# Recurrent attention and a sine feed-forward on one core: turns of three tiles moved next to other small matrix work, fewer output products ahead of phase 1, another order of loads

## The chip, the cores and the metric

One core of a Trainium2 chip runs the kernel. The metric is device time in microseconds (us), the median of several executions; lower is better. Engines are named as in the profile: PE is TensorE (matrix products; PEld its weight loads), DVE is VectorE, ACT is ScalarE, POOL is GpSimd, SP is SyncE, which issues transfers only. GpSimd issues most of the loads as well. PSUM is the memory into which TensorE writes, and a tile there must be emptied before its buffer is used again.

## The reference

```python
gamma = 1.0 - 2.0 ** (-5.0 - np.arange(H))            # B, H, S, D = 4, 8, 768, 64
for t in range(S):
    state = gamma * state + k[:, :, t] (x) v[:, :, t]   # outer product, 64 x 64 per head
    y[:, :, t] = D ** -0.5 * q[:, :, t] @ state
x = y.transpose(0, 2, 1, 3).reshape(3072, 512)
h = x @ w_in                                           # 512 -> 2048
g = h + sin(alpha * h) ** 2 / (alpha + 1e-9)
out = g @ w_out                                        # 2048 -> 512
```

All inputs are float32; the kernel converts them to bfloat16 while they are loaded.

## The kernel before, in words

**Tiles.** The recurrence is computed in chunks of 128 tokens, six for each of the four batch rows, 24 tiles in all. `order` (also `P`) lists them: first the four first chunks (`e0` to `e3`, which need no earlier state), then chunks 1 to 5 of batch row 0 (`P[4]` to `P[8]`), of row 1 (`P[9]` to `P[13]`), and so on. Tiles form ten groups of 4, 2, ..., 2, 4, and the feed-forward takes one group at a time (`sizes`, line 50).

**A tile's attention.** Its q and k are *turned* (transposed) first: by TensorE in `stage_T` (line 259), with one copy out of PSUM by the engine given, or from `P[8]` on by a transfer on SP's queue (`turn`, line 272). Its v is multiplied by decays in place (`scale_v`, line 154). Then comes its *stretch* on TensorE, `burst(old, new)` (line 413): `inter` (q of the old tile times the state in `s_q`), a first round of products over the old tile's own scores and values, the `scores` of the new tile, and a second round, which a `nop` holds back until the first is written (`behind`). Tiles from the middle of row 1 on (`wide`) have another layout: their state products are in `sums` and their own products in `mix`. The stretch leaves closures that other engines run later: `exit` (DVE multiplies the result into `xT`), `keep` (DVE adds to the state `s_f`), `hand` (ACT or POOL copies `s_f` into `s_q` for the next stretch) and `mask` (DVE masks the scores of the new tile into `aT`). `first_state` (line 291) builds the state of batch row 0 behind its first chunk.

**The feed-forward.** `Slot` (line 484) computes some columns of h for a group (16 matmuls of 128 x 128 weights, four for each 128 columns of `d_ff`), ACT takes the sine, `sq` squares it on ACT or DVE, `add` (DVE) writes `gT`. `ff_out` (line 520) accumulates one of 16 products (`po`) of `g @ w_out` for one tile; `take` copies a finished output and SP stores it. `F` calls it for the tiles 0 to 2 of the first group, `fill(n)` takes the next n from a list of 26 products of the tiles 2 and 3 of that group, `outs`; what is left of the list goes into phase 1, spread over its slots.

**Order.** Nothing is scheduled for the author: each engine executes its instructions in the order of the text, and each waits by semaphores for its data. The text runs: loads on POOL's queue (lines 160 to 174 and 615 to 626), the first chunks' attention, phase 0 (lines 675 to 711: slots of the first group, with `F` behind them), a bridge (lines 712 to 762: the attention of `P[4]` and `P[5]`, the turns of `P[4]` to `P[6]`, the rest of `F`, fills, and in the middle POOL's list of later loads and scales), and then `phase(g, ...)` for the groups 1 to 9, in which the stretches and turns are hung at places `(group, slot)`. In phase 1 the turn of `P[7]` hangs at slot 0, the stretches of `P[6]` and `P[7]` at the slots 2 and 5 of eight.

PSUM is shared by tags: `mm` (four buffers: slots, turns, outputs), `pa` (scores) and `two` (one double bank: stretches and, early on, two outputs).

Of the kernel before, what the change touches and what calls it, by code (L numbers as in the profile page):

```python
# [16 lines left out]
def kernel(  # L17
# [15 lines left out]
    nc = tc.nc  # L33
    B, H, S, D = q.shape
    C = 128
    NCH = S // C
# [33 lines left out]
    def half(x):  # L70
        return slice(64 * x, 64 * x + 64)
# [94 lines left out]
    for b in range(2):  # L166
        nc.gpsimd.iota(tok[64 * b:64 * b + 64], pattern=[[C, NCH], [64, 2]], channel_multiplier=1, base=0,
                       allow_small_or_imprecise_dtypes=True)
    load_chunk(order[3], "qk")
    for h in range(2):  # L170
        load_w_out(0, h)
    load_chunk(order[3], "v")
    load_w_in(1)
    load_w_out(1)

# [115 lines left out]
    def first_state(j):  # L291

        ps = psum.tile([128, NP, D], F32, name="ps", tag="mm", bufs=4)
        for b, m, e in heads:
            h = head(b, m, e)
            nc.tensor.matmul(ps[half(e), 2 * b + m, :], raw["k", j][:, h, :], raw["v", j][:, h, :],
                             start=(b == 0 and m == 0), stop=True, skip_group_check=True)
        nc.scalar.copy(s_q[1], ps)
        nc.vector.tensor_copy(s_f, ps)

# [64 lines left out]

    def sums(now, to, lo):

        ks, vs = raw["k", now], raw["v", now]
        for r in range(2):
            for b, m, e in heads:  # L370
                if wide(now):
                    bank, at, kh, vh = b, lo, ks[half(b), r, 2 * m + e, :], vs[half(b), r, 2 * m + e, :]
                else:
                    h, f = head(b, m, e), b ^ r
                    bank, at, vh = f, lo + 128 * r, vs[half(f), h, :]
                    kh = ks[half(f), h, :]
                last = nc.tensor.matmul(to[bank][half(e), at + 64 * m:at + 64 * m + 64], kh, vh,
                                        start=False, stop=True, skip_group_check=True)
        return last
# [33 lines left out]
    def burst(old, new, first=None, apart=False):  # L413
# [4 lines left out]
        if not wide(old):  # L418
            last = round_of(old, now, 0)
        elif now is not None and now is not old:  # L420
            last = sums(now, st["py", old], 256)
        more = scores(new) if new is not None else {}
        py = st["py", old]
        at = [t[:, 256:384] for t in py]
        if wide(old) and now is old:
            pa = st["pa", new]
            at = [pa[:, b, 384:512] for b in range(2)]
            sums(now, [pa[:, b] for b in range(2)], 384)
        rest = tiles4
        if new is None:  # L430
# [17 lines left out]
        def keep():  # L448
            if wide(old) and now is not old:
                nc.vector.tensor_copy(s_f.rearrange("p (b m) d -> p b m d", b=2),  # L450
                                      st["pyw", old][:, :, 256:384].rearrange("p b (m d) -> p b m d", m=2))
                for b in range(2):
                    o = s_f[:, 2 * b:2 * b + 2]
                    nc.vector.tensor_add(o, o, py[1 - b][:, 384:512].rearrange("p (m d) -> p m d", m=2))  # L454
                return
# [157 lines left out]
    for j in (e0, e1):  # L613
        scale_v(j, nc.vector)
    for h in range(2):
        load_w_in(2, h)
    for c in range(1, NCH - 1):
        decay_table(c)
    load_w_out(2)
    for h in range(2):  # L620
        load_w_in(3, h)
    load_chunk(order[4], "qk")
    load_w_out(3)
    load_chunk(order[4], "v")
    for j in order[5:7]:
        load_chunk(j)

# [43 lines left out]
    def fill(n):  # L671
        for _ in range(n):
            outs.pop(0)()
# [14 lines left out]
    c.add()  # L688
    stage_M(e3, psum.tile([128, 2, 512], F32, name="pye", tag="pa")[:, 0])
    d.add()  # L690
    for j in (e2, e3):
        scale_v(j, nc.vector)
    F((0, 1, 2), (2,))
# [4 lines left out]
    for f in range(5, FF):  # L698
# [9 lines left out]
        if f == 9:  # L708
            first_state(e0)
        if f == 13:  # L710
            stage_T(P[4], nc.vector, "pa")
    scale_v(P[4], nc.gpsimd)
    m4 = scores(P[4])["mask"]
    F((0, 1), (13,))
    fill(5)
    stage_T(P[5], nc.scalar, "mm")
    a.add()
    m4()
    fill(3)
    scale_v(P[5], nc.vector)  # L720
    fresh = burst(P[4], P[5], apart=True)
    run(fresh, "keep", "hand", "mask")
    fill(2)
    F((0, 1), (14,))
    F((0, 1), (15,))
    run(fresh, "exit")


    load_chunk(P[7])
    load_chunk(P[8], "qk")  # L730
    scale_v(P[6], nc.gpsimd)
# [3 lines left out]
    load_chunk(P[10], "qk")  # L735
    decay_table(NCH - 1)
    load_chunk(P[9], "v")
    scale_v(P[8], nc.gpsimd)
    load_chunk(P[10], "v")
    load_seq(1, "q")  # L740
    load_seq(1, "k")
    load_seq(1, "v")
    scale_v(P[10], nc.gpsimd)
    load_seq(2, "q")
# [11 lines left out]
    load_seq(3, "v")  # L756

    fill(1)
    stage_T(P[6], nc.scalar, "mm")
    fill(3)  # L760
    run(burst(P[5], P[6]), "exit", "keep", "hand", "mask")
    fill(4)
    where = {7: (1, 2), 8: (1, 5)}
# [12 lines left out]

    at((1, 0), lambda: stage_T(P[7]))
    for n in (8, 9):
        at((1, n - 7), X(P[n]))
    for n in range(7, NJ + 1):  # L780
# [5 lines left out]
        if n >= 19 and n < NJ:  # L786
            at(where[n], lambda j=new: scale_v(j, nc.gpsimd))
    at((2, 3), lambda: scale_v(P[9], nc.vector))
    phase(1, outs, atts[1], 2)
    for g in range(2, NG):  # L790
# [32 lines left out]
```

## Time and profile before

| | us |
|---|---|
| median of three runs | 210.12 (209.93 to 210.23) |
| the profiled execution | 209.51 |
| its span in the profile | 207.7 |
| TensorE busy | 198.0 (95%) |
| VectorE, ScalarE, GpSimd busy | 152.8, 151.5, 116.3 |
| software queue of transfers (GpSimd's) | 92.1% of 16 engines' span |

The page of the profile has the busy times, the span in 40 slices of 5.2 us (a digit is a busy share in tenths), and groups of instructions. A row of a timeline has the start in us, the us that a merged run of like instructions covers, engine, line, operation, output and inputs, shapes and count, and in brackets the idle time before it with what ended it. Matrix products are pipelined, so the next row begins before the covered time of a row is over: the distance of two starts is the cost. The trace lacks a few records of `po` directly behind stretches; an idle time of 0.16 us with "issue" that is printed there is such a missing product.

### The profile page before, as it was taken

The page shows a single profiled execution, that of the slowest core. Times are in us where ns is not written, and L with a number is a line of the kernel's source. Part 1 is how long each engine was busy: PE and PEld are TensorE (multiplying, and loading weights), DVE is VectorE, ACT ScalarE, POOL GpSimd, SP SyncE. Part 2 cuts the span into 40 slices and gives each one's busy share as a digit, 9 for nine tenths or more (in the row PEclk, how much of TensorE's full clock was granted, in tenths as well). Part 3 has the DMA queues.
Part 4 walks back from the last instruction along what each step waited for, and adds up shares of the span by engine and source line. Part 5 has one row for each costly group of instructions (what it writes and reads, how often), then busy time and mean ns, then how long its engine had stood idle before and what let it go on. Part 6 is the DMA issues. An engine that isn't in the chain of part 4 may idle for free.

```text
span 207.7 us, 5741 instructions
## 1 busy us (share of the span) xinstructions
PE 198.0 (95%) x2342; PEld 123.4 (59%) x2370; DVE 152.8 (74%) x314; ACT 151.5 (73%) x309; POOL 116.3 (56%) x157
## 2 busy tenths in 40 slices
PE   7799999999999999999999999999999999999994
PEld 2445544457766666666666666666666654444453
DVE  5789788867989967868878868868888965656220
ACT  7778776657998787687687687686685779999001
POOL 8999956699999999898499932002022300000000
PEclk9999999999999999999999999999999999999999
DMA  8999999999999999999999996421422101010212
GB/s 134 152 181 197 202 200 183 154 168 198 156 161 113 110 189 155 171 103 161 114 141 197 159 172 71 104 70 35 106 63 41 54 2 52 0 50 3 101 50 101
DMA packets 102074, 24.79 MB, mean 119 GB/s; under 512 B 93040, under 2 KB 99104, under 8 KB 102048
## 3 DMA queue, kind: packets, MB, share of 16 engines
q0 software_dynamic: 79248, 13.38, 92.1%
q1 hardware_dynamic: 22656, 10.99, 26.0%
q8 instruction: 18, 0.29, 0.6%
q14 instruction: 8, 0.07, 0.1%
q10 hardware_dynamic: 144, 0.07, 0.1%
HBM read 27.30 MB, written 6.29 MB: 162 GB/s over the span
## 4 chain that ended last, share of the span: by engine, by line
PE 85%; ACT 5%; DVE 3%; DMA 2%; issue 2%; POOL 2%; POOLq 0%; ACTq 0%
PE po L523 37%; PE ph L498 37%; DMA qkr<-in_q_dram 2%; PE py L338 2%; ACT s L501 2%; ACT s L506 2%; PE poh L548 2%; PE py L392 1%; DVE gT L513 1%; DVE aT L288 1%; PE pt L266 1%; POOL vr L100 1%; POOL qkr L100 1%; PE pa L348 1%; PE pa L355 1%
## 5 line engine op out<-in xcount | busy, mean ns | idle before, releaser
L513 DVE SCALAR_TENSOR_TENSOR gT<-s,rec_alpha,ph 128x256 bf16<-128x256 f32 (+3 forms) x164 | 79.9, 523 | 30.9 <-ACT s L506 30.4
L498 PE MATMUL ph<-xT,w_in 128*128 128x256 bf16 (+3 forms) x652 | 98.3, 290 | 0.5 <-issue 0.3
L501 ACT ACTIVATE s<-ph,alpha_sb 128x256 f32<-128x256 f32 (+3 forms) x164 | 76.0, 506 | 29.9 <-PE ph L498 29.9
L523 PE MATMUL po<-w_out,gT 128*128 128x512 bf16 x345 | 90.5, 379 | 3.1 <-issue 2.7
L498 PEld LDWEIGHTS <-w_in 128*128 128x128 bf16 x656 | 63.3, 98 | 33.1 <-issue 1.0
L506 ACT ACTIVATE s<-s 128x512 f32<-128x512 f32 (+1 forms) x91 | 56.9, 625 | 2.9
L523 PEld LDWEIGHTS <-gT 128*128 128x128 bf16 x368 | 34.0, 98 | 30.3 <-DVE gT L513 0.2
L535 DVE COPY o_sb<-po 128x512 f32<-128x512 f32 x20 | 13.8, 690 | 10.3 <-PE po L523 9.8
L469 POOL CAST s_q<-s_f 128x256 bf16<-128x256 f32 x5 | 2.0, 396 | 34.2 <-DVE s_f L454 17.8
L120 POOL DMA_DIRECT2D qk_seq<-in_q_dram x24 | 17.0, 808 | 3.5 <-DMA v_seq<-in_v_dram 3.4
L120 POOL DMA_DIRECT2D qk_seq<-in_k_dram x24 | 17.1, 779 | 1.1 <-DMA qk_seq<-in_q_dram 0.7
L120 POOL DMA_DIRECT2D v_seq<-in_v_dram x24 | 16.9, 802 | 0.0
L158 POOL TENSOR_TENSOR v_seq<-v_seq,kgq 128x512 bf16<-128x512 bf16 x13 | 13.7, 1075 | 3.8 <-DMA v_seq<-in_v_dram 3.8
L443 DVE TENSOR_TENSOR xT<-py,qg 128x512 bf16<-128x512 f32 x19 | 13.0, 684 | 0.6 <-PE py L408 0.6
L363 DVE TENSOR_TENSOR aTw<-pa,maskq 128x768 bf16<-128x768 f32 x13 | 12.4, 952 | 0.0
L100 POOL DMA_DIRECT2D vr<-in_v_dram x11 | 10.2, 929 | 0.9 <-DMA w_in<-in_moe_w_in_dram 0.5
L552 ACT COPY o_sb<-poh 128x256 f32<-128x256 f32 (+1 forms) x2 | 0.6, 319 | 11.7 <-PE poh L548 11.2
L568 PE MATMUL spare<-warm 128*128 128x512 bf16 x24 | 7.7, 450 | 1.2 <-DVE warm L178 1.2
L351 DVE TENSOR_TENSOR aT<-pa,mask 128x1024 bf16<-128x1024 f32 x7 | 8.5, 1219 | 0.0
L469 ACT CAST s_q<-s_f 128x256 bf16<-128x256 f32 x14 | 5.5, 391 | 3.3 <-DVE s_f L463 3.0
L158 POOL TENSOR_TENSOR vr<-vr,kg 128x512 bf16<-128x512 bf16 x5 | 5.6, 1126 | 2.9 <-DMA vr<-in_v_dram 2.8
L100 POOL DMA_DIRECT2D qkr<-in_k_dram x7 | 6.3, 898 | 1.7 <-DMA w_out<-in_moe_w_out_dram 1.7
(101 smaller groups left out, 162.1 us busy)
## 6 DMA issues: line engine op xcount, KB each, us to landing
out_dram<-o_sb SPq DMA_DIRECT2D x23, 256.0 KB, 3.7
w_in<-in_moe_w_in_dram POOLq DMA_DIRECT2D x6, 256.0 KB, 9.9
w_out<-in_moe_w_out_dram POOLq DMA_DIRECT2D x3, 512.0 KB, 10.5
vr<-in_v_dram POOLq DMA_DIRECT2D x11, 128.0 KB, 5.4
qk_seq<-in_q_dram POOLq DMA_DIRECT2D x16, 80.0 KB, 7.8
qk_seq<-in_k_dram POOLq DMA_DIRECT2D x16, 80.0 KB, 5.6
v_seq<-in_v_dram POOLq DMA_DIRECT2D x16, 80.0 KB, 5.1
qkr<-in_q_dram POOLq DMA_DIRECT2D x7, 128.0 KB, 5.3
```

Source lines behind the costliest of these rows:

```text
L100: nc.gpsimd.dma_start(out=t, in_=chunk_of(src, j))
L120: nc.gpsimd.dma_start(out=o, in_=src[bt, head(b, m, e), cs[0] * C:, :].rearrange("(f i) d -> i f d", i=64))
L158: eng.tensor_mul(t, t, by[:, j % NCH, :, None].to_broadcast([128, H, D]))
L351: return {"mask": lambda: nc.vector.tensor_mul(aT.rearrange("p e n t -> p (e n) t"), pa.rearrange("p e (n t) -> p (e n) t", n=NP), mask_bc)}
L363: return {"mask": lambda: nc.vector.tensor_mul(aT, pa[:, :, 0:384].rearrange("p e (m t) -> p e m t", m=2), maskq[:, None, None, :].to_broa ...
L443: nc.vector.tensor_mul(o, st["pyw", old][:, :, 0:256].rearrange("p b (m t) -> p b m t", m=2), by)
L498: nc.tensor.matmul(self.ph[:, m, :], w_in[:, i, f * 128:(f + 1) * 128], xT[g][:, i, self.lo:self.hi], start=(m == 0 and i == 0), stop=(i = ...
L501: nc.scalar.activation(out=self.s[:, m, :], in_=self.ph[:, m, :], func=ACTF.Sin, scale=alpha_sb[:, f:f + 1])
L506: nc.scalar.activation(out=self.s, in_=self.s, func=ACTF.Square)
L513: nc.vector.scalar_tensor_tensor(gT[self.g][:, f, self.lo:self.hi], self.s[:, m, :], rec_alpha[:, f:f + 1], self.ph[:, m, :], op0=ALU.mult ...
L523: nc.tensor.matmul(po[g, ts], gT[g][:, f, ts * C:(ts + 1) * C], w_out[:, f, :], start=(f == 0), stop=(f == FF - 1))
L535: nc.vector.tensor_copy(o_sb, po[g, ts])
```

## The change

- **Loads.** `w_out`'s first half, then the v of `e3`, then the other half; the second quarters of both weights and the third of `w_in` in halves, in turn. The fifth decay table is built with the other four. The last quarter of `w_out` goes ahead of `P[4]`; the q and k of `P[5]` and `P[6]` go ahead of their v. The q and k of `P[7]` and `P[8]` are issued ahead of the scale of `P[5]`, the v of `P[7]` behind it.
- **First state.** Its eight products stand behind `stage_M(e3)`, its two copies behind `d.add()`; `scale_v(e3)` takes the old place at slot 9.
- **Turns.** `P[4]`'s goes from slot 13 to the end of phase 0; `P[5]`'s stands directly behind `P[4]`'s scores, `P[6]`'s and `P[7]`'s directly behind the stretches of `P[4]` and `P[5]`, all three copied by ACT.
- **Fills.** 11 of the 26 products are taken ahead of phase 1 instead of 18.
- **Scales.** `P[5]`'s goes from DVE to POOL, `P[10]`'s from POOL to DVE (phase 3, slot 0).
- **Rounds.** Where a `wide` stretch crosses into the next batch row, half of the first-state products go behind the scores, into the scores' PSUM tile.

```diff
@@ -167,11 +167,14 @@
         nc.gpsimd.iota(tok[64 * b:64 * b + 64], pattern=[[C, NCH], [64, 2]], channel_multiplier=1, base=0,
                        allow_small_or_imprecise_dtypes=True)
     load_chunk(order[3], "qk")
+    load_w_out(0, 0)
+    load_chunk(order[3], "v")
+    load_w_out(0, 1)
     for h in range(2):
-        load_w_out(0, h)
-    load_chunk(order[3], "v")
-    load_w_in(1)
-    load_w_out(1)
+        load_w_in(1, h)
+    for h in range(2):
+        load_w_out(1, h)
+        load_w_in(2, h)
     warm = consts.tile([128, 512], BF16, name="warm")
@@ -289,14 +292,16 @@
-        nc.scalar.copy(s_q[1], ps)
-        nc.vector.tensor_copy(s_f, ps)
+        def copies():
+            nc.scalar.copy(s_q[1], ps)
+            nc.vector.tensor_copy(s_f, ps)
+        return copies
@@ -363,16 +368,16 @@
-    def sums(now, to, lo):
+    def sums(now, to, lo, rs=(0, 1)):
...
-        for r in range(2):
+        for r in rs:
...
-                    bank, at, vh = f, lo + 128 * r, vs[half(f), h, :]
+                    bank, at, vh = f, lo, vs[half(f), h, :]
@@ -418,7 +423,7 @@
-            last = sums(now, st["py", old], 256)
+            last = sums(now, st["py", old], 256, (0,))
@@ -426,6 +431,8 @@
+        elif wide(old) and now is not None:
+            sums(now, [st["pa", new][:, b] for b in range(2)], 384, (1,))
@@ -451,7 +458,7 @@
-                    nc.vector.tensor_add(o, o, py[1 - b][:, 384:512].rearrange("p (m d) -> p m d", m=2))
+                    nc.vector.tensor_add(o, o, st["pa", new][:, 1 - b, 384:512].rearrange("p (m d) -> p m d", m=2))
@@ -612,18 +619,17 @@
     later_mask()
     for j in (e0, e1):
         scale_v(j, nc.vector)
-    for h in range(2):
-        load_w_in(2, h)
-    for c in range(1, NCH - 1):
+    for c in range(1, NCH):
         decay_table(c)
     load_w_out(2)
     for h in range(2):
         load_w_in(3, h)
-    load_chunk(order[4], "qk")
     load_w_out(3)
-    load_chunk(order[4], "v")
+    load_chunk(order[4])
     for j in order[5:7]:
-        load_chunk(j)
+        load_chunk(j, "qk")
+    for j in order[5:7]:
+        load_chunk(j, "v")
     rest = [{}]
@@ -687,9 +693,10 @@
     F((0, 1, 2), (0, 1))
     c.add()
     stage_M(e3, psum.tile([128, 2, 512], F32, name="pye", tag="pa")[:, 0])
+    copies = first_state(e0)
     d.add()
-    for j in (e2, e3):
-        scale_v(j, nc.vector)
+    copies()
+    scale_v(e2, nc.vector)
     F((0, 1, 2), (2,))
     a = Slot(0, 0, (n3, n4), 4, "pa")
     F((0, 1, 2), (3,))
@@ -706,41 +713,38 @@
         if f > 6:
             F((0, 1, 2) if f < 9 else (0, 1), (f - 3,))
         if f == 9:
-            first_state(e0)
-        if f == 13:
-            stage_T(P[4], nc.vector, "pa")
+            scale_v(e3, nc.vector)
     scale_v(P[4], nc.gpsimd)
+    load_chunk(P[7], "qk")
+    load_chunk(P[8], "qk")
+    stage_T(P[4], nc.vector, "pa")
+    F((0, 1), (13,))
+    fill(4)
+    a.add()
     m4 = scores(P[4])["mask"]
-    F((0, 1), (13,))
-    fill(5)
     stage_T(P[5], nc.scalar, "mm")
-    a.add()
     m4()
-    fill(3)
-    scale_v(P[5], nc.vector)
-    fresh = burst(P[4], P[5], apart=True)
-    run(fresh, "keep", "hand", "mask")
-    fill(2)
     F((0, 1), (14,))
     F((0, 1), (15,))
-    run(fresh, "exit")
-    load_chunk(P[7])
-    load_chunk(P[8], "qk")
+    fill(1)
+    scale_v(P[5], nc.gpsimd)
+    fresh = burst(P[4], P[5], apart=True)
+    stage_T(P[6], nc.scalar, "mm")
+    run(fresh, "keep", "hand", "mask", "exit")
+    load_chunk(P[7], "v")
     scale_v(P[6], nc.gpsimd)
     load_chunk(P[9], "qk")
     load_chunk(P[8], "v")
     scale_v(P[7], nc.gpsimd)
     load_chunk(P[10], "qk")
-    decay_table(NCH - 1)
     load_chunk(P[9], "v")
     scale_v(P[8], nc.gpsimd)
-    load_chunk(P[10], "v")
     load_seq(1, "q")
     load_seq(1, "k")
+    load_chunk(P[10], "v")
     load_seq(1, "v")
-    scale_v(P[10], nc.gpsimd)
     load_seq(2, "q")
     scale_v(P[11], nc.gpsimd)
     load_seq(2, "k")
@@ -755,11 +759,11 @@
         scale_v(j, nc.gpsimd)
     load_seq(3, "v")
+    fill(5)
+    fresh = burst(P[5], P[6])
+    stage_T(P[7], nc.scalar, "mm")
+    run(fresh, "exit", "keep", "hand", "mask")
     fill(1)
-    stage_T(P[6], nc.scalar, "mm")
-    fill(3)
-    run(burst(P[5], P[6]), "exit", "keep", "hand", "mask")
-    fill(4)
     where = {7: (1, 2), 8: (1, 5)}
     for g in range(2, NG - 1):
         first = P.index(groups[g + 1][0])
@@ -774,7 +778,6 @@
-    at((1, 0), lambda: stage_T(P[7]))
@@ -786,6 +789,7 @@
+    at((3, 0), lambda: scale_v(P[10], nc.vector))
```

## The prediction

> **What bounds the kernel now.** I read the page first, then TensorE's own waits, then the chain of waits for the price of one matrix instruction, then the timelines of TensorE and GpSimd from 14 to 61 us, where every edit but one falls.
>
> ```profile
> span 207.7 us, 5741 instructions
> ...
> PE 198.0 (95%) x2342; PEld 123.4 (59%) x2370; DVE 152.8 (74%) x314; ACT 151.5 (73%) x309; POOL 116.3 (56%) x157
> ...
> DMA  8999999999999999999999996421422101010212
> ```
>
> TensorE is busy for 198.0 of 207.7 us, so a gain must take away matrix work or one of its few gaps. The DMA row says something else about the first quarter: from the second slice on, the transfer engines are full for over 100 us. A load there lands when the bytes ahead of it have gone through, whatever the time of its issue.
>
> ```profile
> 5.06 4.85 DMA qkr<-in_q_dram
> ...
> 19.51 0.53 DVE gT L513
> ...
> 71.38 0.87 PE ph L498 x8
> ...
> 190.47 9.28 PE po L523 x43
> ```
>
> From the chain: a 256-column `ph` costs 0.87/8 = 0.109 us, a `po` 9.28/43 = 0.216 us. A pair of rows that lies further apart than these prices hides a wait even where no idle time is printed. That is how the next rows are read.
>
> **The change, part by part.** The profiled execution took 209.51 us (span 207.7, 1.8 around it); the median shown is 210.12, 0.6 above. I sum against 209.51 and add the 0.6 at the end.
>
> *First state beside stage_M.*
>
> ```profile
> 19.59 0.41 PE L314 MATMUL pye<-aT,vr 128*64 128x128 bf16 x8
> 20.09 0.82 PE L523 MATMUL po<-w_out,gT 128*128 128x512 bf16 x3
> ...
> 29.32 0.32 PE L296 MATMUL ps<-vr,kb 128*64 128x64 bf16 x8
> 29.57 1.04 PE L498 MATMUL ph<-xT,w_in 128*128 128x512 bf16 x4
> ```
>
> The `po` at 20.09 waited for VectorE's add, 19.51 + 0.53 = 20.04. The eight `ps` matmuls take 29.57 - 29.32 = 0.25 us, and 0.09 to enter (below). Behind `stage_M`, in the same 128*64 shape, they fill that wait, which costs nothing; if the wait were gone they would cost 0.25 there. The gain is 0.34 at 29 us (bounds 0.09 and 0.34). ScalarE's and VectorE's two copies move with them into a stretch where VectorE also loses one `scale_v`.
>
> *Turns next to scores and stretches.*
>
> ```profile
> 40.08 0.64 PE L266 MATMUL pt<-ident,qkr 128*64 128x128 bf16 x16
> ...
> 45.42 0.28 PE L401 MATMUL py<-aT,vr 64*64 64x128 bf16 x8
> 45.48 0.28 PE L408 MATMUL py<-vr,qkr 64*64 64x64 bf16 x8
> 45.70 0.42 PE L348 MATMUL pa<-qkT 64*64 64x128 bf16 x16
> ...
> 47.17 1.03 PE L498 MATMUL ph<-xT,w_in 128*128 128x256 bf16 x8
> 48.13 0.64 PE L266 MATMUL pt<-ident,qkr 128*64 128x128 bf16 x16
> 48.70 0.39 PE L523 MATMUL po<-w_out,gT 128*128 128x512 bf16 x1
> ```
>
> Eight `ph` from 47.17 end at 48.04, the turn starts at 48.13: 0.09 to enter. The turn then holds TensorE 0.57, so a turn on its own costs 0.66. Merged, it drops the entry and the exit of one of the two (taken as long as an entry, for want of a row), 0.18 for each of three; no row shows 64*64 followed by 128*64, so the saving lies between 0 and 0.18. The Trainium skill ("TensorEngine Tiling (Array Packing)", Key Properties) says that changing the tiling mode drains TensorE, so a turn behind a stretch would still pay one drain, and three merges would give about 0.27 instead of 0.54 us.
>
> In that second stretch eight L401 matmuls took 0.06, the eight L408 behind them 0.22: the scores of P[6] (45.70) had to wait for ScalarE's copy of its turn, which was only just out (44.64 + 1.01 = 45.65):
>
> ```profile
> 42.98 0.40 ACT L469 CAST s_q<-s_f 128x256 bf16<-128x256 f32 x1 [1.20 <-DVE s_f L463]
> ...
> 44.64 1.01 ACT L268 COPY qkT<-pt 128x1024 bf16<-128x1024 bf16 x1 [0.20 <-PE pt L266]
> ```
>
> That is a hidden wait of about 0.12, and it goes, as the turn moves ahead.
>
> *What is late next.* These savings count only if TensorE need not wait for loads and scaled values.
>
> ```profile
> 16.77 4.03 POOL L231 TENSOR_TENSOR qg<-qg,step 128x512 f32<-128x512 f32 x4
> 20.75 0.82 POOL L135 DMA_DIRECT2D w_out<-in_moe_w_out_dram  x1
> ...
> 27.50 0.87 POOL L100 DMA_DIRECT2D qkr<-in_q_dram  x1 [0.43 <-DMA w_in<-in_moe_w_in_dram]
> 30.05 0.87 POOL L100 DMA_DIRECT2D qkr<-in_k_dram  x1 [1.67 <-DMA w_out<-in_moe_w_out_dram]
> ...
> 38.23 1.04 POOL L158 TENSOR_TENSOR vr<-vr,kg 128x512 bf16<-128x512 bf16 x1 [2.85 <-DMA vr<-in_v_dram]
> ...
> 41.01 0.90 POOL L100 DMA_DIRECT2D vr<-in_v_dram  x1
> 41.88 1.53 POOL L98 DMA_DIRECT2D qkr<-in_q_dram  x2
> 43.35 1.54 POOL L98 DMA_DIRECT2D qkr<-in_k_dram  x2
> 44.84 1.12 POOL L158 TENSOR_TENSOR vr<-vr,kg 128x512 bf16<-128x512 bf16 x1
> ```
>
> ```profile
> qkr<-in_k_dram POOLq DMA_DIRECT2D x1, 128.0 KB, 10.0
> ```
>
> The k of P[5] (issued at 30.05) lands 10.0 us later, at 40.05; its turn ran at 40.08. In the changed order exactly the same loads precede it (all weights, P[4], its own q), so with full transfer engines it lands at 40.05 again. TensorE would come to that turn at 40.08 - 0.34 (first state) - 0.22 (one `po` fewer ahead) - about 0.1 (scores joined) = 39.4 and wait 0.6 us. The first gains are lost there.
>
> The second gate is GpSimd. The v of P[4] lands at 38.23, again behind the same loads. Then GpSimd scales it, issues q and k of P[7] and the four pieces of P[8], and only then scales P[5], which VectorE did before. Before, the v of P[7] stood between (41.88 - 41.01 = 0.87) and the scale behind the four pieces began at 44.84: now it begins at 43.97 and ends at 45.09 (bounds 45.0 and 45.3 by other durations of this operation, 1.04 and 1.31). The second stretch's round over P[5]'s values can start at 45.15; in the run before it started at 45.42. What is queued behind it on TensorE is the whole rest, since it executes in order. TensorE would be there at about 44.5: the T[5] turn at 40.08 holds it 0.57, five `po` 1.08, the stretch about 0.9 (below: 1.75 less four `po` and the wait, and 0.14 ahead of its round), the turn 0.57, five `po` 1.08, entries 0.2. ScalarE gives nearly the same limit: P[6]'s turn is copied (1.01) ahead of the state's hand-over (0.40), from about 43.3 to 44.7.
>
> From that round to the first slot of phase 1 it was 47.17 - 45.42 = 1.75 us, of it 0.12 the wait for the copy; the rest hangs on VectorE's exit and stays. So phase 1 begins at 45.15 + 1.63 = 46.78, 0.39 sooner.
>
> *What phase 1 then carries.* Fifteen `po` instead of eight: + 7 x 0.216 = 1.51. Its turn at slot 0 is gone: -0.66. Its gaps:
>
> ```profile
> 57.60 2.14 PE L498 MATMUL ph<-xT,w_in 128*128 128x256 bf16 x16
> 59.63 1.02 PE L523 MATMUL po<-w_out,gT 128*128 128x512 bf16 x4
> 60.62 1.03 PE L498 MATMUL ph<-xT,w_in 128*128 128x256 bf16 x8
> ```
>
> Sixteen `ph` should take 1.74 and took 2.03; four `po` 0.86 and took 0.99. These 0.42 us are ScalarE's pace at the end of phase 1; with 1.5 us more of `po` between the slots and sines that start 0.4 sooner they go: -0.42 (bounds 0 and 0.42).
>
> *First-state rounds apart*, in the two stretches that cross into a new batch row.
>
> ```profile
> 101.23 0.20 PE L359 MATMUL pa<-qkT 64*64 64x64 bf16 x4
> 101.45 0.37 PE L392 MATMUL py<-aTw,v_seq 64*64 64x128 bf16 x16
> ```
>
> The mix begins 0.22 after the last scores have begun, although four such matmuls take 0.03: it waits until the sums are written. With half of the sums (eight of 16, 0.06) behind the scores, that half covers part of the wait: -0.06 each, -0.12 for both (bounds 0 and -0.4).
>
> *Moved at no cost:* `scale_v(e3)` to the tenth slot of phase 0 (VectorE idles there), P[10]'s scale from GpSimd to VectorE one slot before its stretch, the v of P[7] and P[10] later on GpSimd's queue by 4 and 1 us, still several us ahead of their rounds. If one of these covers failed, it would cost the 0.7 us of one scale.
>
> *The sum:* -0.39 + 1.51 - 0.66 - 0.42 - 0.12 = -0.08 us, so 209.4 for the profiled execution and **210.0** as a median.
>
> **The rivals.** *A, the forecast: the gates hold.* Its own range: the landing of P[4]'s v moves everything one to one; I allow half a transfer of 128 KB (0.87 by the spacing 41.88 - 41.01) to either side, 0.45, and the bounds above: 209.5 to 210.7.
>
> *B, the gates lie earlier and the covers do their work.* Then TensorE's own sum decides: -0.34 (first state), -0.12 (the wait for the copy), -0.54 (three merges), -0.42, -0.12 = -1.54, that is 208.6. It needs P[5]'s k 0.65 us sooner, and its scaled v well over 1 us sooner. For it: loads that are cut finer and reordered could run better than in the profile, and the turn at 40.08 shows that P[5] was already at the limit, so each tenth sooner counts in full. Against it: the full DMA row. Half of it, 209.3, is as likely as all.
>
> *C, slower: the transfer queue runs dry behind the decay tables.* Weights in halves mean two more issues (0.75 each) ahead of the tables, and the tables are five instead of four (1.0 each): the next weight is issued at 20.75 + 2.5 = 23.3. What is queued by then lasts until the second half of `w_in`'s third quarter has landed, about 27.3 (the issue at 27.50 had waited for it), so 4.0 us. A load with some others ahead took 4.85 from issue to landing at the start of the run. If a new issue needs more than 4.0 us, the rest leaves a hole, up to 0.85 us, which shifts P[4]'s v, P[5]'s k and so everything behind: 210.9. It decides from a hole of 0.5 on. Against it: before, an equal pause in issues left no dip in the DMA row. The Trainium skill ("DMA: Bandwidth & Descriptors", Anatomy of one DMA) gives about 2.0 us of fixed time for such a load, by which the queue would not run dry and C would be out.
>
> **How the numbers follow.** A 0.42, B 0.32, C 0.26. What a measurement here can tell is about 0.2%, 0.42 us. A is faster by more in some 0.08, slower in 0.03, the same in the rest: faster 0.40, same 0.31, slower 0.29. The range leaves out the far end of B and what lies above C's price: 208.9 to 211.0.
>
> **What would show it.** Right: the turn of P[5] starts within 0.3 us of 40.08 with TensorE idle ahead of it, the scale of P[5] on GpSimd ends near 45.1, the first slot of phase 1 starts near 46.8 and phase 2 near 58.8, with no gap at the end of phase 1; `ps` runs near 19.9 without moving the `po` behind it. B: phase 1 starts before 46.2. C: GpSimd's first scale starts after 38.7, or a slice with a DMA digit under 9 near 25 us. I would be wrong in kind if phase 2 or later showed new gaps, since I see no stage behind 61 us that any of this reaches but the two crossings.

## The result and the profile after

The changed kernel takes **211.42 us** (median of 14 executions, 210.23 to 212.24); the kernel before, on the same chip, 209.88 (14 executions, 209.60 to 211.01). The ratio is 1.0061, 95% interval 1.0045 to 1.0077: 0.6% slower. The profiled execution took 210.84 us with a span of 209.0, so the two profiles lie 1.33 us apart and the medians 1.54.

From the page of the changed kernel, the busy times, the rows of the transfers and the shares of the chain:

```profile
span 209.0 us, 5768 instructions
...
PE 201.9 (97%) x2370; PEld 124.2 (59%) x2370; DVE 152.6 (73%) x313; ACT 152.2 (73%) x310; POOL 118.2 (57%) x159
...
DMA  8999999999999999999999994412412101010212
GB/s 131 155 183 193 196 172 182 155 204 160 121 140 167 108 199 171 173 103 183 173 118 171 158 147 53 103 52 52 105 52 51 53 2 52 0 50 3 100 50 100
...
PE 76%; POOL 16%; DMA 5%; issue 1%; DVE 0%; POOLq 0%
```

The digits of the DMA row have not moved where it matters: nines from the second slice on. The row below them has. The sixth slice (26.1 to 31.3 us) moved 172 GB/s; the same slice of the kernel before:

```profile
GB/s 134 152 181 197 202 200 183 154 168 198 156 161 113 110 189 155 171 103 161 114 141 197 159 172 71 104 70 35 106 63 41 54 2 52 0 50 3 101 50 101
...
PE 85%; ACT 5%; DVE 3%; DMA 2%; issue 2%; POOL 2%; POOLq 0%; ACTq 0%
```

It moved 200. And the chain that ended last, which before ran for 85% of the span on TensorE, now runs for 16% of it over GpSimd and for 5% over a load of v: TensorE came to wait for them. Cut finer, by stretches (the last three columns are granted clock, DMA share and GB/s; the fifth pair is GpSimd), after and then before:

```profile
26.00:27.00 1.00, 1.00 (x6) 0.40 (x6) 1.00 (x2) 0.97 (x3) 1.00 (x2) 1.00 1.00 132
27.00:31.00 4.00, 4.00 (x20) 1.82 (x19) 3.93 (x7) 2.85 (x5) 4.00 (x6) 1.00 1.27 181
```

```profile
26.00:27.00 1.00, 1.00 (x6) 0.48 (x5) 0.96 (x3) 1.00 (x2) 0.81 (x2) 1.00 1.28 206
27.00:31.00 4.00, 4.00 (x27) 1.79 (x25) 3.50 (x6) 2.81 (x6) 1.82 (x3) 1.00 1.36 200
```

The DMA share adds up the times of packets that overlap and goes above 1 (GpSimd's queue alone comes to 1.57 between 17 and 38.2 us of the kernel before), so a digit of 9 doesn't say that the transfers are at their full rate: 1.00 with 132 GB/s prints the same 9 as 1.28 with 206. In these five microseconds 74 + 4 x 19 = 150 KB less were moved, 0.75 us at 200 GB/s. In the second stretch GpSimd was busy for all of 4.00 us, issuing. That the issues held the transfers back there is not shown: four pieces of weights, 1536 KB, had been issued by 27.14 and landed only between 30.27 and 36.59. Why the rate was 181 stays open.

GpSimd's timeline in the changed kernel shows where the hole comes from and where it goes:

```profile
17.82 0.77 POOL L131 DMA_DIRECT2D w_in<-in_moe_w_in_dram  x1 [0.40 <-DMA w_out<-in_moe_w_out_dram]
18.67 5.48 POOL L234 TENSOR_TENSOR qg<-qg,step 128x512 f32<-128x512 f32 x5
24.09 0.81 POOL L135 DMA_DIRECT2D w_out<-in_moe_w_out_dram  x1
...
32.04 0.88 POOL L100 DMA_DIRECT2D qkr<-in_q_dram  x1 [0.52 <-DMA w_in<-in_moe_w_in_dram]
33.40 0.87 POOL L100 DMA_DIRECT2D qkr<-in_k_dram  x1 [0.49 <-DMA w_in<-in_moe_w_in_dram]
36.88 1.77 POOL L100 DMA_DIRECT2D vr<-in_v_dram  x2 [2.60 <-DMA w_out<-in_moe_w_out_dram]
39.49 1.04 POOL L158 TENSOR_TENSOR vr<-vr,kg 128x512 bf16<-128x512 bf16 x1 [0.84 <-DMA vr<-in_v_dram]
...
45.24 1.10 POOL L158 TENSOR_TENSOR vr<-vr,kg 128x512 bf16<-128x512 bf16 x1
```

The issue at 17.82 takes until 18.59, and between 18.59 and 24.09 nothing is issued. The v of `P[4]` is there to be scaled at 39.49 instead of 38.23, 1.26 later; `P[5]`'s scale ends at 46.34. TensorE's timeline carries that on:

```profile
40.26 0.42 PE L353 MATMUL pa<-qkT 64*64 64x128 bf16 x16
40.61 0.41 PE L269 MATMUL pt<-ident,qkr 128*64 128x128 bf16 x8
41.29 0.41 PE L269 MATMUL pt<-ident,qkr 128*64 128x128 bf16 x8 [0.26 <-DMA qkr<-in_k_dram]
...
45.72 0.31 PE L343 MATMUL py<-qkT,s_q 64*64 64x128 bf16 x8 [0.23 <-ACT s_q L476]
46.40 0.30 PE L406 MATMUL py<-aT,vr 64*64 64x128 bf16 x8 [0.37 <-POOL vr L158]
...
48.08 1.05 PE L505 MATMUL ph<-xT,w_in 128*128 128x256 bf16 x8
...
59.37 1.91 PE L505 MATMUL ph<-xT,w_in 128*128 128x256 bf16 x16
61.11 1.03 PE L530 MATMUL po<-w_out,gT 128*128 128x512 bf16 x4
```

The turn of `P[5]` stops in the middle for its k, the second stretch waits for the hand-over and then for the scaled v, and the first slot of phase 1 begins at 48.08 (before: 47.17).

### The profile page after: what moved, and what is told of

It reads as the page before. It is cut to its first block, busy times and chain, and to the rows that moved or that the text cites. A ratio compares the mean times of both kernels' runs of the same rounds, so it can differ in the third digit from the quotient of the medians.

```text
span 209.0 us, 5768 instructions
## 1 busy us (share of the span) xinstructions
PE 201.9 (97%) x2370; PEld 124.2 (59%) x2370; DVE 152.6 (73%) x313; ACT 152.2 (73%) x310; POOL 118.2 (57%) x159
## 4 chain that ended last, share of the span: by engine, by line
PE 76%; POOL 16%; DMA 5%; issue 1%; DVE 0%; POOLq 0%
PE po L530 34%; PE ph L505 33%; DMA vr<-in_v_dram 5%; POOL qkr L100 4%; POOL w_in L131 3%; POOL qg L234 3%; POOL w_out L135 2%; PE py L343 2%; POOL vr L100 2%; PE poh L555 2%; POOL qkr L98 1%; PE py L397 1%; POOL vr L158 1%; PE py L406 1%; PE pa L360 1%; PE pa L382 1%
## 5 line engine op out<-in xcount | busy, mean ns | idle before, releaser
L508 ACT ACTIVATE s<-ph,alpha_sb 128x256 f32<-128x256 f32 (+3 forms) x164 | 76.1, 506 | 29.2 <-PE ph L505 29.2
L530 PE MATMUL po<-w_out,gT 128*128 128x512 bf16 x368 | 95.2, 380 | 0.0
L575 PE MATMUL spare<-warm 128*128 128x512 bf16 x25 | 8.8, 475 | 1.2 <-DVE warm L181 1.2
L271 ACT COPY qkT<-pt 128x1024 bf16<-128x1024 bf16 x3 | 3.0, 1012 | 5.4 <-PE pt L269 5.4
L100 POOL DMA_DIRECT2D qkr<-in_q_dram x7 | 6.4, 918 | 0.5 <-DMA w_in<-in_moe_w_in_dram 0.5
```

The lines of the kernel that those rows point to most:

```text
L100: nc.gpsimd.dma_start(out=t, in_=chunk_of(src, j))
L508: nc.scalar.activation(out=self.s[:, m, :], in_=self.ph[:, m, :], func=ACTF.Sin, scale=alpha_sb[:, f:f + 1])
L530: nc.tensor.matmul(po[g, ts], gT[g][:, f, ts * C:(ts + 1) * C], w_out[:, f, :], start=(f == 0), stop=(f == FF - 1))
L575: nc.tensor.matmul(spare["ps"], warm[:, :128], warm, start=True, stop=True)
```

## The experiments

Two theories stood at the start. **D**: the transfer queue runs dry behind the decay tables, because halves fill it with more issues for the same bytes and the fifth table lengthens the pause; all that is late follows from it. **G**: GpSimd's own order is the cause, the scale of `P[5]` moved onto it behind six issues. The expectations name two more: **S**, the first slot of the changed kernel's profile began at 15.41 instead of 14.66, and that is carried to the end; **H**, smaller loads lose transfer time by themselves. The ratios below are to the kernel before, on the same chip, with 95% intervals.

**1. The changed kernel, the five tables behind the loads of `P[4]`.**

```diff
-    for c in range(1, NCH):
-        decay_table(c)
     load_w_out(2)
...
     load_chunk(order[4])
+    for c in range(1, NCH):
+        decay_table(c)
```

> The changed kernel with its five decay tables moved on GpSimd's queue from ahead of the third quarter of w_out to behind P[4]'s loads; nothing else. Theory D (the transfer queue runs dry while GpSimd computes tables: third quarter of w_out issued at 24.1 us instead of 20.8): it is issued near 18.7, the transfers lose no rate at 26 to 31 us, GpSimd's scale of P[4] starts at 38.3 or sooner (39.49 in the changed kernel), phase 1 begins 1.2 us sooner, at about 46.8, and the time is back at the kernel before's, ratio 0.998 to 1.001. Rival G (the gate is GpSimd's scale of P[5] behind six issues, whatever the landing): P[4]'s v lands sooner, but the time stays at +0.8 us or more. Rival S (the changed kernel's first slot began 0.76 us later, at 15.4, and that is carried to the end): no change, ratio 1.006.

Measured: 211.30 us, 1.0045 (1.0025 to 1.0065). The gain did not come. GpSimd's timeline and the stretches of the transfers:

```profile
21.37 0.74 POOL L131 DMA_DIRECT2D w_in<-in_moe_w_in_dram  x1 [0.56 <-DMA w_out<-in_moe_w_out_dram]
...
28.87 6.34 POOL L234 TENSOR_TENSOR qg<-qg,step 128x512 f32<-128x512 f32 x5
35.17 0.94 POOL L100 DMA_DIRECT2D qkr<-in_q_dram  x1
...
40.46 1.10 POOL L158 TENSOR_TENSOR vr<-vr,kg 128x512 bf16<-128x512 bf16 x1
```

```profile
26.00:27.00 1.00, 1.00 (x6) 0.41 (x5) 1.00 (x3) 1.00 (x2) 0.59 (x2) 1.00 1.32 205
...
36.00:40.00 4.00, 3.40 (x29) 1.66 (x29) 3.34 (x6) 2.63 (x5) 4.00 (x6) 1.00 1.72 110
```

The first hole is gone (205 GB/s), and a larger one stands behind the tables in their new place: 110 GB/s from 36 to 40 us, where the kernel before and the changed one both have 155. The hole follows the tables. (This profile comes from an execution of 212.47 us, 1.2 above the median of the run.) The row at 21.37 shows something else: with nothing between the issues, a load still waits, for an earlier load. The semaphore events say which. Every load has one of eight semaphores, in turn, and has landed with the last of sixteen increments; a load is issued only once the load eight places before it, which has the same semaphore, has landed, 0.3 us after it. In the changed kernel, `P[6]`'s q was issued at 32.04 (the eighth before it landed at 31.75), its k at 33.40 (33.12), the first v at 36.88 (36.59). **With its eight semaphores this program has at most eight loads in flight**, so nothing can be issued far ahead to bridge a pause, and a half takes the same place as a whole. Whether the queue itself would hold more, no run here shows.

**2. The kernel before, with the changed order and size of the early loads and five tables early,** nothing else.

```diff
-    for h in range(2):
-        load_w_out(0, h)
+    load_w_out(0, 0)
     load_chunk(order[3], "v")
-    load_w_in(1)
-    load_w_out(1)
+    load_w_out(0, 1)
+    for h in range(2):
+        load_w_in(1, h)
+    for h in range(2):
+        load_w_out(1, h)
+        load_w_in(2, h)
...
-    for h in range(2):
-        load_w_in(2, h)
-    for c in range(1, NCH - 1):
+    for c in range(1, NCH):
         decay_table(c)
...
-    decay_table(NCH - 1)
```

> The kernel before with one part of the change alone: the early order of loads (v of e3 between the halves of w_out's first quarter, second quarters in halves, third quarter of w_in ahead of the tables) and all five decay tables ahead of the third quarter of w_out. Theory D: the transfers fall behind here too; P[5]'s k, which landed at 40.05 right ahead of its turn at 40.08, lands about 1.2 us later, TensorE waits there, ratio 1.003 to 1.006. Rival G: the kernel before scales P[5] on VectorE and is not gated; ratio within 0.001 of 1.

Measured: 211.33 us, 1.0052 (1.0032 to 1.0071). The early loads and the fifth table, without the moved scale, make most of the loss:

```profile
20.18 6.37 POOL L234 TENSOR_TENSOR qg<-qg,step 128x512 f32<-128x512 f32 x5
26.50 0.81 POOL L135 DMA_DIRECT2D w_out<-in_moe_w_out_dram  x1
...
41.26 1.04 POOL L158 TENSOR_TENSOR vr<-vr,kg 128x512 bf16<-128x512 bf16 x1 [2.26 <-DMA vr<-in_v_dram]
```

```profile
26.00:27.00 1.00, 0.34 (x2) 0.10 (x1) 1.00 (x5) 1.00 (x2) 1.00 (x2) 1.00 0.68 95
27.00:28.00 1.00, 0.95 (x5) 0.45 (x5) 1.00 (x2) 0.73 (x3) 1.00 (x2) 1.00 0.20 28
28.00:29.00 1.00, 1.00 (x6) 0.43 (x5) 0.96 (x3) 0.61 (x1) 1.00 (x3) 1.00 0.87 39
```

The next issue comes at 26.50 here, and for two microseconds the transfers nearly stand still. D holds in the kernel before as well. (The profiled execution took 212.42 us, 1.1 above the median, so this hole is larger than the usual one.)

**3 and 4. The changed kernel, the fifth table late again; and with `P[5]`'s scale on VectorE again.**

```diff
-    for c in range(1, NCH):
+    for c in range(1, NCH - 1):
         decay_table(c)
...
     load_chunk(P[10], "qk")
+    decay_table(NCH - 1)
```

```diff
-    scale_v(P[5], nc.gpsimd)
+    scale_v(P[5], nc.vector)
```

> The changed kernel with the fifth decay table alone back at its old place, behind P[10]'s q and k. Theory D, by dose: the third quarter of w_out is issued 1.1 us sooner, at 23.0; the part of the dip that this covers is gained, a third to all of it: 0.4 to 1.2 us faster than the changed kernel, ratio 1.000 to 1.004. Rival G: P[4]'s v sooner but no gain, ratio 1.006.

> The changed kernel with P[5]'s scale on VectorE as before, ahead of the stretch of P[4] in VectorE's order; the tables stay. Theory D with the gate on GpSimd only as its last link: the second stretch's round no longer waits for 46.3, but P[5]'s v lands at about 43 and ScalarE hands the state over at 45.7, so it gains 0.5 us at most, and VectorE, which waits for that v in order, delays keep and mask: 0 to 0.5 us faster than the changed kernel, ratio 1.004 to 1.006. Rival G: the gate is gone, ratio 1.001 or less.

Measured: 210.45 us, 1.0019 (0.9998 to 1.0039) with the fifth table late, about two thirds of the loss taken back; 211.76 us, 1.0069 (1.0048 to 1.0091) with the scale on VectorE, nothing gained. G is out as the cause.

**5. The changed kernel, the tables singly between the loads.**

```diff
-    for c in range(1, NCH):
-        decay_table(c)
     load_w_out(2)
+    decay_table(1)
     for h in range(2):
         load_w_in(3, h)
+        decay_table(2 + h)
     load_w_out(3)
+    decay_table(4)
     load_chunk(order[4])
+    decay_table(5)
```

> The changed kernel with its five decay tables spread singly between the loads that follow (behind w_out's third quarter, behind each half of w_in's last, behind w_out's last, behind P[4]), so that GpSimd never leaves the queue for more than one table; order and size of the loads as changed. Theory D (the five tables in one go, 5.5 to 6.4 us, outlast what the eight loads in flight hold): no dip in the transfer rate, scale of P[4] starts at 38.0 to 38.6, scale of P[5] ends near 45.2, phase 1 begins near 46.9, ratio 0.998 to 1.002. Rival H (the smaller loads lose transfer time by themselves, wherever the tables stand): scale of P[4] at 39 or later, ratio 1.003 or more. Rival G (gate on GpSimd only): ratio 1.004 or more with the scale of P[4] at 38.3.

Measured: 210.88 us, 1.0015 (0.9994 to 1.0037). The rate held (204 GB/s from 26 to 27 us), yet the first scale began at 39.71, so the expectation missed. H is not borne out either: its sign, a scale at 39 or later, came, but the rate was that of the kernel before (204 and 200 GB/s from 26 to 27 and from 27 to 31 us, there 206 and 200). S is not borne out: here the first slot began at 14.70 and phase 1 still at 48.31, and in the changed kernel TensorE stood idle ahead of both gates. Two things stand in their place. TensorE lost time at 25 us, behind VectorE:

```profile
21.29 2.01 DVE L158 TENSOR_TENSOR vr<-vr,kg 128x512 bf16<-128x512 bf16 x1
23.22 1.96 DVE L515 TENSOR_TENSOR s<-s 128x512 f32<-128x512 f32 x1
...
26.39 1.02 PE L505 MATMUL ph<-xT,w_in 128*128 128x512 bf16 x4 [1.32 <-DVE gT L520]
```

These two operations take 0.68 and 0.69 us in run 6 below, where no table runs beside them. The Trainium skill ("SBUF — State Buffer", Who interferes with whom) says that a VectorE instruction with two inputs in SBUF contends with a GpSimd instruction that reads SBUF, and that the ports they share are locked exclusively. The rows agree as far as they go: the two operations took 1.33 and 1.27 us longer, somewhat more than one table of 1.04 to 1.14.

And the v landed late though the bytes kept up. The spread of a load's sixteen increments differs from profile to profile (from the semaphore events, for the v of `P[4]`):

```
kernel     landed   first to last increment
before     38.15    1.71
after      39.41    1.56
run 5      39.64    2.92
run 6      38.78    2.13
```

In run 5 the first of the sixteen came almost 3 us ahead of the last. Why, the trace doesn't show, and it stays open. In the changed kernel the spread was smaller than before: what it lost was lost ahead of the first increment (37.86, before 36.44).

**6. The changed kernel with the early loads as before:** whole quarters, their old order, four tables, the fifth late. All other parts stay (the last quarter ahead of `P[4]`, q and k of `P[5]` and `P[6]` ahead of their v, turns, fills, first state, scales, rounds).

```diff
-    load_w_out(0, 0)
-    load_chunk(order[3], "v")
-    load_w_out(0, 1)
-    for h in range(2):
-        load_w_in(1, h)
     for h in range(2):
-        load_w_out(1, h)
-        load_w_in(2, h)
+        load_w_out(0, h)
+    load_chunk(order[3], "v")
+    load_w_in(1)
+    load_w_out(1)
...
-    for c in range(1, NCH):
+    for h in range(2):
+        load_w_in(2, h)
+    for c in range(1, NCH - 1):
         decay_table(c)
...
+    decay_table(NCH - 1)
```

> The changed kernel with the early loads as in the kernel before: second quarters of both weights whole, third quarter of w_in ahead of four tables, fifth table late; all else as changed. Theory D: the eight loads in flight hold enough again, scale of P[4] at 38.3, ratio 0.998 to 1.002. Rival H: the same. Rival G: ratio 1.004 or more.

Measured: 210.09 us, 0.9992 (0.9964 to 1.0020): no difference from the kernel before that can be told, and 0.7%, about 1.4 us, under the changed kernel by the two ratios. The two profiled executions lie 0.73 apart (210.11 and 210.84).

```profile
26.00:27.00 1.00, 1.00 (x7) 0.46 (x5) 0.96 (x2) 0.97 (x3) 0.56 (x2) 1.00 1.34 206
```

```profile
38.86 1.04 POOL L158 TENSOR_TENSOR vr<-vr,kg 128x512 bf16<-128x512 bf16 x1 [0.86 <-DMA vr<-in_v_dram]
...
44.62 1.10 POOL L158 TENSOR_TENSOR vr<-vr,kg 128x512 bf16<-128x512 bf16 x1
```

```profile
40.63 0.41 PE L266 MATMUL pt<-ident,qkr 128*64 128x128 bf16 x8 [0.28 <-DMA qkr<-in_k_dram]
...
45.77 0.30 PE L403 MATMUL py<-aT,vr 64*64 64x128 bf16 x8 [0.39 <-POOL vr L158]
...
47.45 1.05 PE L502 MATMUL ph<-xT,w_in 128*128 128x256 bf16 x8
```

No hole, and the two gates still hold: TensorE waits for `P[5]`'s k and for its scaled v. These are the gates of the forecast's case A, some 0.65 us later than it had them.

**7. Run 5 with GpSimd's and ScalarE's gates moved ahead:** q of `P[7]` issued ahead of `P[4]`'s scale, the hand-over ahead of `P[6]`'s copy.

```diff
+    load_chunk(P[7], "q")
     scale_v(P[4], nc.gpsimd)
-    load_chunk(P[7], "qk")
+    load_chunk(P[7], "k")
...
+    run(fresh, "keep", "hand")
     stage_T(P[6], nc.scalar, "mm")
-    run(fresh, "keep", "hand", "mask", "exit")
+    run(fresh, "mask", "exit")
```

> e5 with two more moves: q of P[7] issued ahead of the scale of P[4], in the time in which GpSimd waits for that v, so that the scale of P[5] ends 0.9 us sooner, near 44.3; and ScalarE hands the state over ahead of its copy of P[6]'s turn. Theory D with the gates of the prediction: the second stretch's round starts at 44.6 instead of 45.2, ratio 0.3% below that of e5: 0.995 to 0.999. If TensorE's own work or the landing of P[5]'s k decides instead: as e5.

Measured: 210.41 us, 1.0007 (0.9987 to 1.0028). The waits of the second stretch went, but TensorE still lost 1.3 us behind VectorE at 25 us, as in run 5, and phase 1 began at 48.06.

**8 and 11. The fifth table early, in the kernel before and in run 6.**

```diff
-    for c in range(1, NCH - 1):
+    for c in range(1, NCH):
         decay_table(c)
...
-    decay_table(NCH - 1)
```

> The kernel before with one edit: the fifth decay table computed with the other four. Theory D, as a dose: GpSimd leaves the queue for 5.0 instead of 4.0 us, with whole quarters of the weights in flight (10.5 us of transfers at the start of the pause): no dip, ratio 0.999 to 1.001. If the fifth table alone were the cause: ratio 1.003 or more.

> e6 with the fifth table early again, so that of the early part only the weights' pieces differ from the changed kernel: whole quarters with five tables. With halves it was 1.006 with five tables and 1.002 with four; whole with four 0.999. Theory D (what eight loads in flight hold must outlast the tables; whole quarters hold enough for both): ratio 0.997 to 1.002. If the fifth table decides alone: 1.004 or more.

Measured: 209.93 us, 0.9979 (0.9952 to 1.0006) in the kernel before, 209.99 us, 1.0010 (0.9986 to 1.0034) in run 6. With whole quarters the longer pause costs nothing that can be told. In the changed kernel it does: halves and five tables 1.0061, halves and four 1.0019, whole and five 1.0010, whole and four 0.9992. The loss comes mainly from both together, though the intervals of about 0.002 to either side don't bar a small cost of each. The runs 6 and 11 put back the whole quarters and the old order of the early loads together, so the size and the order are not told apart. Counted by the rows, the tables begin 1.90 us later with the halves (18.67 after 16.77) and the five take 1.45 longer than the four (5.48 and 4.03).

What tells these runs apart is the time by which the issue of `w_out`'s third quarter (512 KB) leads the landing of the last piece queued ahead of the tables (issues and GB/s by the profiles, first and last increment of that piece from the semaphore events):

```
kernel   issued   first   last    lead   GB/s in the 1 us from 26, 27, 28
before   20.75    26.12   27.22   6.5    206  209  197
run 11   22.06    26.29   28.04   6.0    204  203  204
run 8    22.19    26.38   27.66   5.5    202  209  201
run 3    24.12    26.42   28.60   4.5    169  187  196
after    24.09    26.08   27.57   3.5    132  193  178
run 4    25.10    26.61   28.16   3.1    149   77  201
run 2    26.50    26.26   29.09   2.6     95   28   39
```

From a lead of five and a half down, the hole grows steadily. It begins with the first increment, which comes between 26.1 and 26.6 in every row, and not with the last: in the changed kernel the half microseconds from 25.5 on have 181, 109 and 156 GB/s. And it ends some 2.7 us after the issue: in run 2 the half microseconds from 28.5 on have 22, 98 and 211 GB/s, in run 4 those from 27.0 on 57, 96 and 199. Run 4 and the changed kernel have the same early loads and tables, so their two rows also show how far executions of one order differ. (The profiled executions of the runs 2, 3 and 4 took 212.42, 211.26 and 211.48 us, their medians are 211.33, 210.45 and 211.76.)

**9, 10 and 12. Run 6, its waits filled or moved.** In run 9 six products instead of four stand ahead of `P[4]`'s scores and eight instead of five behind `P[6]`'s turn. Runs 10 and 12 take the six, and the two moves of run 7; the last fill is five in run 10 and three in run 12.

```diff
-    fill(4)
+    fill(6)
...
-    fill(5)
+    fill(8)
```

> e6 (early loads as before, the rest as changed) with five output products taken out of phase 1 and put where TensorE waited in e6: six instead of four ahead of P[4]'s scores (0.45 us of wait for P[5]'s k), eight instead of five behind P[6]'s turn (0.86 us of wait for the state and for P[5]'s scaled values). Theory D with the prediction's gates: phase 1 begins as in e6, at 47.4, and carries 5 x 0.216 = 1.08 us less; some of ScalarE's gap of 0.42 at its end may return: 0.7 to 1.1 us faster than e6, ratio 0.994 to 0.997. If no gate holds TensorE there: as e6.

> e6 with two more products ahead of P[4]'s scores and the two moves of e7 (q of P[7] issued in the time in which GpSimd waits for P[4]'s v; the state handed over ahead of the copy of P[6]'s turn). Theory D with the gates: the waits of 0.45 and 0.86 us go, phase 1 begins about 0.8 us sooner than in e6 with two products less to carry: 0.9 to 1.3 us faster than e6, ratio 0.993 to 0.996. If TensorE's own work decides already: as e6.

> e10 with three instead of five products behind P[6]'s turn, so that only the ten products of the third output stand ahead of the second stretch: the eleventh opens a new PSUM buffer, and in e10 TensorE waited there 0.7 us for ScalarE's copy of P[6]'s turn. As in e6, eleven are taken ahead of phase 1. Theory D with the gates: no wait at that place, the second stretch's round starts as soon as P[5]'s scale is done, 0.9 us sooner than in e6 (near 44.9 where P[4]'s v lands as in e6), ratio 0.994 to 0.997. If the two moves gain nothing: as e6, 0.999.

Measured: run 9 209.83 us, **0.9982 (0.9968 to 0.9996)**; run 10 210.05 us, 1.0005 (0.9982 to 1.0027); run 12 209.71 us, **0.9983 (0.9969 to 0.9997)**. Run 9's wait is new, a product that opens a new PSUM buffer of the tag `mm`, which `P[6]`'s turn still held:

```profile
PE po L527 <- ACT qkT L268: 0.4, 1, 0.4
```

(TensorE's waits: microseconds in all, times, longest.) Run 10 had the same for 0.7 us (in its slowest execution, 211.94). Run 12 stays below that buffer, and gets the earlier scale it was made for; then another resource is late:

```profile
43.41 1.09 POOL L158 TENSOR_TENSOR vr<-vr,kg 128x512 bf16<-128x512 bf16 x1
```

```profile
56.31 0.42 PE L350 MATMUL pa<-qkT 64*64 64x128 bf16 x16 [1.04 <-DMA qkT<-qkr]
```

```profile
48.62 10.15 SPq L275 DMA_TRANSPOSE qkT<-qkr  x3
```

`P[5]`'s scale began 1.2 us sooner than in run 6 (0.35 of it because `P[4]`'s did, at 38.51), phase 1 at 46.34 instead of 47.45, and the stretch of `P[7]` then waited 1.04 us for `P[8]`, which SP's queue turns behind its loads. At the end of phase 1 nothing of it was left: the sixteen `ph` that lead into phase 2 began at 58.80, in run 6 at 58.73. Expected had been 0.994 to 0.997. The runs 9 and 12 are the only versions here that are faster than the kernel before beyond the interval, by 0.2%; with upper ends of 0.9996 and 0.9997, in twelve comparisons, that is little, and against run 6 no gain can be told.

## Why the prediction was wrong, step by step

The forecast was 210.0 us, the range 208.9 to 211.0: the time lies 0.4 above it, and rival C, at 0.26, is what happened.

**The step that failed** is "so with full transfer engines it lands at 40.05 again", said of the k of `P[5]`, and with it "The v of P[4] lands at 38.23, again behind the same loads". The k landed at 41.24, and the v was scaled from 39.49 on. The loads ahead are the same, the transfer engines were not full: 132 GB/s from 26 to 27 us instead of 206. "Full" was read from the digits of the DMA row, which can't show it; the row of GB/s can.

The hole is not the whole delay in the profiles. Run 6, which has none, has the scale of `P[4]` at 38.86 and phase 1 at 47.45 in place of 46.78: of the 1.26 us, run 6 takes back 0.63 and keeps 0.63, a little over the 0.45 that A allowed. The other profiles with these early loads have the scale at 38.51 (run 12), 38.76 (run 11) and 39.03 (run 9), all behind 38.23, by 0.28 to 0.80; run 10's 41.19 is from its slowest execution. What makes this second part is not shown.

**C's price** was mis-sized in the time of the issue. It was put at 23.3; it was 24.09. Two parts were missing: 0.40 us of waiting for one of eight places (17.82), and the tables, 5.48 us for five in place of 5.0. With 24.09, C's own rule, 4.85 us from issue to landing less the lead, gives 4.85 - (27.57 - 24.09) = 1.37 us, and the scale of `P[4]` was 1.26 late. That they agree is partly luck: by the bytes the hole was 0.75 us, by run 6 0.63, and the rule starts the hole at the last increment (27.57), while the rate fell from the first on (26.08). Of C's two signs the first came, a scale after 38.7, though run 6 has it without a hole; the second, a digit under 9, could not show.

**C's chance** was set low by two arguments. The first was that an equal pause had left no dip. The pause before was 4.03, with a lead of 27.22 - 20.75 = 6.5 us by the landings; runs 8 and 11 show that pauses of 5.48 and 5.04 are still covered there. It was no evidence for a lead of 3.5. The second: the Trainium skill ("DMA: Bandwidth & Descriptors", Anatomy of one DMA) gives about 2.0 us of fixed time for such a load, completion included. The runs don't contradict it: in the runs 2 and 4 the issue ended at 27.31 and 25.91, and the rate was back at about 29.2 and 27.8, 1.9 us later. But the prediction set it against the last increment of what was queued; the first came 1.49 us sooner, at 26.08, when the issue at 24.09 could not carry yet.

**What was late followed the model of the gates.** The round of the second stretch was expected at 45.15 and came at 46.40, phase 1 at 46.78 and came at 48.08, phase 2 at 58.8 and came at 59.37 + 0.87 = 60.24: 1.25, 1.30 and 1.44 late, for a v that was 1.26 late. "The landing of P[4]'s v moves everything one to one" held.

**Three small terms** can be seen in their places:

```profile
20.32 0.41 PE L319 MATMUL pye<-aT,vr 128*64 128x128 bf16 x8
20.56 0.30 PE L298 MATMUL ps<-vr,kb 128*64 128x64 bf16 x8
20.84 0.82 PE L530 MATMUL po<-w_out,gT 128*128 128x512 bf16 x3
```

From `pye` to the `po` behind it 0.52 us with the first state in between, 0.50 before without it: `ps` costs 0.02 there, as forecast. At the end of phase 1 the sixteen `ph` take 61.11 - 59.37 = 1.74 us where they had taken 2.03: the gap went. The crossing stretch:

```profile
102.19 0.31 PE L343 MATMUL py<-qkT,s_q 64*64 64x128 bf16 x8
...
102.75 0.37 PE L397 MATMUL py<-aTw,v_seq 64*64 64x128 bf16 x16
```

takes 0.56 from its first row to its mix, 101.45 - 100.83 = 0.62 before: the 0.06 that were forecast. The merged turns were hidden behind the gates, so what they save in time was not tested. But the entry that a merge was to drop is still there: sixteen scores cost 0.25 us before (45.70 to 45.95), and the turn behind them begins 0.35 after them (40.26 to 40.61), so it pays 0.10, about as much as the 0.09 of a turn on its own.

Run 6 has all of these terms and ends at 0.9992 of the kernel before; the forecast, 210.0 to 210.12, is 0.9994. That doesn't confirm the sum: the interval of run 6 is 0.3% to either side, 0.6 us, far more than the 0.08 us of the sum, and its profiled execution, 210.11, lies 0.7 above the 209.4 that the sum gives for one, as its phase 1 is 0.67 late.

## What to carry to other kernels

A program that allows a fixed number of loads in flight fills its queue by count, not by bytes: before a load is cut into halves, ask how many microseconds of bytes will be queued when the issuing engine next turns to other work, and compare the next issue with the time when the queued bytes begin to run out, the first increment of the last piece, not its landing (here a lead of 5.5 us over the landing left no dip, 4.5 left one). Judge whether transfers are saturated by the GB/s in narrow windows, not by a digit of busy share. Where a chain of gates lies within a microsecond of each other, removing one hands the time to the next (here a scaled v, then a PSUM buffer, then a turn by transfer), so a gain of 1.1 us at the start of phase 1 was gone at its end.

## What the hardware showed that was not expected

- A load that has to wait for a semaphore is issued 0.3 us after the landing of the load eight places before it, which has the same semaphore (32.04 after 31.75).
- The queue ran out gradually: in the changed kernel the rate fell from about the first increment of the last piece on, 1.5 us ahead of its landing (26.08 and 27.57), and a new issue brought it back only some 2.7 us after its start (runs 2 and 4).
- Two VectorE operations with both inputs in SBUF took 2.0 instead of 0.7 us beside GpSimd's tables (run 5), and a table took 1.27 us (run 1, 6.34 for five) where it took 1.01 in the kernel before.
- The sixteen increments of the v of `P[4]` came 1.6 to 2.9 us apart in the four profiles listed; in run 5, with 2.9, it landed 1.5 us later than in the kernel before, while its first increment was only 0.3 later (36.72 after 36.44).
